# The first heads of a fused attention and mixture-of-experts kernel: another order of score products, zeroings on GpSimd, and a first head scored from 64 rows

## The chip, the cores and the metric

The kernel runs on one core of one Trainium2 chip. A core has TensorE (PE: matrix products and transposes, with a weight load ahead of each), VectorE (DVE), ScalarE (ACT), GpSimd (POOL) and SyncE (SP, which issues most transfers). The metric is the device time of one execution in microseconds, as a median of several executions; lower is better.

## What is computed

The reference, cut to what matters: causal attention of 4 batches with 12 heads, 448 rows and 64 columns a head, and then a mixture of 8 experts over the 1792 rows of 768 that come out.

```python
scores = scale * np.matmul(q, k.transpose(0, 1, 3, 2))
mask = np.triu(np.ones((seq, seq), dtype=bool), k=1)
scores = np.where(mask, -1000000000.0, scores)
scores = scores - np.max(scores, axis=-1, keepdims=True)
attn = np.exp(scores)
attn = attn / (np.sum(attn, axis=-1, keepdims=True) + 1e-09)
x = np.matmul(attn, v)                     # then rows of 768 for the experts
...
logits = x @ w_gate + modality_bias[modality_id]
e_idx = np.argmax(logits, axis=1)          # one expert for each row
out[mask] = gate_w[mask, None] * (np.maximum(x[mask] @ w1[e], 0.0) @ w2[e])
```

## The kernel before

The attention is a pipeline over 48 heads that is written out by hand: `iteration(n)` issues, in program order, the scores of head n, the exponentials of head n-1, the transposes and the split of head n-2, the second product of head n-3 and the sum of its two parts for head n-4. Each engine runs its own instructions in that order and waits for the others by semaphores. Heads come in pairs m = n // 2 (one load of q and k holds two heads, 64 rows each) and in groups of 4 (one load of V).

**Two kinds of heads.** Most heads are split into a high and a low part on GpSimd and stacked by transfers (`split_qk`, `split_kl`, `stack_qk`). The first eight, and the last two, are "plain": `first_load` brings q and k as they are, and the scores are computed with 128 rows, where q's rows of the other head of the pair are zeros. Those zeros are written ahead (`first_view(m, a)` is head a's q of pair m). A plain product runs as two passes.

**Scores.** `st_scores` computes four blocks of query rows: 64, 128, 128 and 128 rows with 64, 192, 320 and 448 columns, numbers 0 to 3. `SPOS` puts blocks 3 and 0 into bank `sa`, blocks 1 and 2 into bank `sb`. There is one bank of each, so a head can write `sa` only when DVE has taken up the head before. `SORD` is the order of the products: 3, 1, 0, 2 for plain heads. `ORD` is the order in which DVE takes the blocks (mask and row maximum, written to `p`): 3, 0, 1, 2. The exponentials on ACT follow DVE block by block.

**Second product.** `st_split` copies the transposed probabilities on ACT (`ph`) and takes the rest on DVE (`pl`); `st_pv` begins with two products of `ph` and goes on with those of `pl`. V is split as well: `split_vh` on GpSimd, `split_vl` for the first group on DVE and for the others on GpSimd. Groups 0 and 1 of V use the same buffer `vraw`, so `load_v(1)` waits until group 0 is split.

**The rest of the start.** 32 warm-up products of ones precede the first head on PE. Zeroings are shared out between DVE and GpSimd; some are put off into the first iterations by `later(n, f)`: `xg`, and parts of `sl` and `lt`. `clear_tables` issues four transfers of 160 KB. All transfers but the first half of q go through SyncE's queue, in program order, and each waits by its semaphore until the one eight issues ahead of it has landed.

Of the kernel before, what the change touches and what calls it, by code (L numbers as in the profile page):

```python
# [21 lines left out]
def attention_moe(  # L22
# [11 lines left out]
    nc = tc.nc  # L34
    V = nc.vector
    P = nc.gpsimd
    A = nc.scalar
    B, HP, _, _, S = qk.shape
# [3 lines left out]
    E, _, DF = w1.shape  # L42
# [3 lines left out]
    GH = 4  # L46
# [28 lines left out]
    def bank(tag, bufs=1):  # L75
        return ps.tile([128, 512], F32, tag=tag, name=tag, bufs=bufs)

    def sm(shape, tag, dt=F32, bufs=2):
        return small.tile(shape, dt, tag=tag, name=tag, bufs=bufs)

    def cst(name, shape, dt=F32):
        return const.tile(shape, dt, name=name)
# [16 lines left out]
    lts = [ltp[:, j] for j in range(2)]  # L99
    sls, pes = ([cst(f"{x}{j}", [128, NTL, E + 1]) for j in range(2)] for x in ("sl", "pe"))  # L100
# [31 lines left out]
    xg = [early.tile([128, DM], F32, name=f"xg{j}") for j in range(2)]  # L132
# [18 lines left out]
    def T(shape, dt, tag, bufs):  # L151
        return atp.tile(shape, dt, tag=tag, name=tag, bufs=bufs)
# [27 lines left out]
    raw, spl, vhl, sc, prob, pt, xrow, rec, lt_all, cx, rt, ov, ol = ({} for _ in range(13))  # L180
# [43 lines left out]
    def first_view(m, c):  # L224
        k, j = (
            ((3, 0), (3, 1), (4, 0)), ((2, 0), (2, 1), (4, 1)),
            ((0, 0), (0, 1), (1, 0)), ((5, 0), (5, 1), (1, 1)),
        )[m][c]
        return raw1[k][:, j * S:(j + 1) * S]

    def first_load(m):
        nc.sync.dma_start(out=first_view(m, 2), in_=qk[0, m, :, 1])
        for a in range(2):
            r = slice(a * 64, a * 64 + 64)
            (nc.sync if m or a else nc.scalar).dma_start(out=first_view(m, a)[r], in_=qk[0, m, r, 0])
            spl[2 * m + a] = (first_view(m, a), first_view(m, 2), None, None)

    LATE = (23,)

# [15 lines left out]
    def v_of(gr):  # L255
        return vraws[gr > 1 and gr % 2 == 0]

    def load_v(gr):
        b, u = divmod(gr, NG)
        c = slice(u * GH * D, (u + 1) * GH * D)  # L260
        t = v_of(gr)
        nc.sync.dma_start(out=t[:, 0:3, :], in_=v[b, 0:384, c].rearrange("(t p) c -> p t c", p=128))
        nc.sync.dma_start(out=t[64:128, 3, :], in_=v[b, 384:448, c])

    def vsrc(gr):
        return v_of(gr).rearrange("p t (h d) -> p t h d", h=GH)

    def split_vh(gr):
        t = T([128, NTL, GH, 2, D], F32R, "vhl", 2)
        P.tensor_scalar(out=t[:, :, :, 0], in0=vsrc(gr), scalar1=1.0, scalar2=0.0, op0=ALU.mult, op1=ALU.add)  # L270
        vhl[gr] = t

    def split_vl(gr, eng):
        t = vhl[gr]
        eng.tensor_tensor(out=t[:, :, :, 1], in0=vsrc(gr), in1=t[:, :, :, 0].bitcast(F32), op=ALU.subtract)

    SPOS = [(0, 448), (1, 0), (1, 192), (0, 0)]
    ORD = (3, 0, 1, 2)
    SORD = ((3, 0), (3, 1), (1, 0), (0, 0), (0, 1), (1, 1), (2, 0), (2, 1))

    def st_scores(g):
        qs, ks, qh, kl = spl.pop(g)
        banks = [bank("sa"), bank("sb")]
        nm = sm([128, NTL], "nm")
        p = praw[g % 3]

        outs, parts = {}, []
        for i, last in SORD:
            q0, n = QT[i]
            w = q0 + n  # L290
            bk, c0 = SPOS[i]
            if not last:
                outs[i] = banks[bk][:n, c0:c0 + w]
            if last and qh is None:
                continue
            a, z = (qh, kl) if last else (qs, ks)
            r = 128 if qh is None else n
            z0 = (128, 64, 64, 0)[i]
            nc.tensor.matmul(
                banks[bk][:r, c0:c0 + w], lhsT=a[:, q0:q0 + r], rhs=z[:, z0:z0 + w],  # L300
                start=(last == 0), stop=(last == 1 or qh is None),
            )
        for i in ORD:
            n = QT[i][1]
            w = QT[i][0] + n
            parts.append((i, n, outs[i], masks[i][:n], p[:n, POFF[i]:POFF[i] + w]))
        for i, n, o, m, z in parts:
            V.tensor_tensor_reduce(  # L308
                out=z, in0=o, in1=m, scale=-scale, scalar=3.0e38, op0=ALU.add, op1=ALU.min,
                accum_out=nm[:n, i:i + 1],  # L310
            )
        sc[g] = (p, parts, nm)
# [143 lines left out]
    def st_norm(gr, i):  # L456
        norm_l(gr, i)
        norm_x(gr, i)
# [472 lines left out]
    with tc.manual_schedule():  # L931
        for m in range(2):
            first_load(m)
# [5 lines left out]
            out=bias_sb.rearrange("p m o e -> p (m o e)"),  # L939
            in_=mod_bias.rearrange("(o m) e -> o (m e)", o=1).to_broadcast([128, NM * E]),  # L940
# [1 line left out]

        V.memset(ones, 1.0)
        warm_bank = bank("x")
        for _ in range(32):
            nc.tensor.matmul(warm_bank[:, 0:128], lhsT=ones, rhs=ones, start=True, stop=True)
        warm = sm([1, 1], "warm")
        V.memset(warm, 0.0)
        for m in range(3):
            for a in range(2):  # L950
                (P if m == 2 else V).memset(first_view(m, a)[64 - a * 64:128 - a * 64], 0.0)
        A.activation(out=warm, in_=warm, func=AF.Exp)
        P.memset(mask12, 0.0)
        P.affine_select(
            out=mask12[:, 384:512], in_=mask12[:, 384:512], compare_op=ALU.is_ge, fill=-1e9,
# [55 lines left out]
        def later(n, f):  # L1011
            todo.setdefault(n, []).append(f)
# [9 lines left out]
                f()  # L1022

        for j in range(2):
            later(2 * j, lambda j=j: V.memset(xg[j], 0.0))
            later(1 + j, lambda j=j: V.memset(sls[j][64:128, 0, E:E + 1], 1.0e6))
            later(1 + j, lambda j=j: V.memset(lts[j][64:128, 0], 0.0))

        def fma(o, x, mul, add):
            P.tensor_scalar(out=o, in0=x, scalar1=mul, scalar2=add, op0=ALU.mult, op1=ALU.add)  # L1030
# [120 lines left out]
        def iteration(n):  # L1151
            split = 7 < n + 3 < NHEAD and n + 3 >> 1 not in LATE
            ahead = n + 5 >> 1 in LATE
            if n % 2 == 1 and split and not ahead:
                stack_qk((n + 3) // 2)
            gr, i = divmod(n - 2 * GH, GH)
            comb = 0 <= gr < B * NG
            if 0 <= n - 4 < NHEAD:
                st_out(n - 4)
            if comb:  # L1160
                st_move(gr, i)
                st_norm(gr, i)
                b, u = divmod(gr, NG)
                if u == NG - 1:
                    later(n + 1, lambda i=i: x_store(b, i))
                    if i == NTL - 1:
                        after_batch(b, n)
            run_todo((n,))
            if n in (2, 3):
                st_trans(n - 2)  # L1170
            if n < NHEAD:
                st_scores(n)
            if n % 2 == 1 and ahead:
                late_load((n + 5) // 2)
                stack_qk((n + 3) // 2)
            run_todo(n)
            if n == 0:
                split_vh(0)
            if n % 2 == 1 and split:
                split_kl((n + 3) // 2)  # L1180
            if n % 2 == 0 and 7 < n + 4 < NHEAD:
                (late_zeros if n + 4 >> 1 in LATE else split_qk)((n + 4) // 2)
            if n % GH == 1 and n > GH:
                st_sums(n // GH - 1)
            if n % GH == RECAT and n > GH:
                st_rec(n // GH - 1)
            if 0 <= n - 1 < NHEAD:
                st_exp(n - 1)
            if 0 <= n - 2 < NHEAD:
                if n > 3:  # L1190
                    st_trans(n - 2)
                run_todo(-n)
                st_split(n - 2)
            if 0 <= n - 3 < NHEAD:
                st_pv(n - 3)
                st_low(n - 3)
            gr, i = divmod(n - 2 * GH + 1, GH)
            if 0 <= gr < B * NG:
                st_comb(gr, i)
            if n == 1:  # L1200
                split_vl(0, V)
            if n == 2 or n % GH == 3 and n > GH and n // GH + 1 < B * NG:
                split_vh(n // GH + 1)
            if n == 2 or n % GH == 0 and n > GH:
                split_vl((n + 2) // GH, P)
            if n == 4:
                V.memset(vraws[1][0:64, 3, :], 0.0)
            if n in (1, 3, 5, 7):
                load_qk(4 + n // 2)
            if n % 2 == 0 and n > 7 and n + 8 < NHEAD and n + 8 >> 1 not in LATE:  # L1210
                load_qk((n + 8) // 2)
            if n in (1, 4):
                load_v(n // GH + 1)
            if n == 1:
                clear_tables()
            if n % GH == 2 and n > GH and n // GH + 2 < B * NG:
                load_v(n // GH + 2)
# [51 lines left out]
        n = NHEAD  # L1269
# [263 lines left out]
```

## Time and profile before

| | |
|---|---|
| median of 3 runs | 483.30 us |
| lowest, highest | 483.16, 484.15 us |
| the profiled execution | 483.15 us |
| its span (first to last instruction) | 481.4 us |
| PE busy in the span | 466.1 us (97%) |
| DVE, ACT, GpSimd busy | 291.1, 278.0, 236.3 us |

A profile is one execution. Busy time of PE is modelled from pipelined products, so two neighbouring products overlap in the rows; what a product costs is read from start to start. A row of the timeline merges equal instructions in a row and says at its end how long the engine was idle before it, if it was, and what the idle time is put down to.

### The profile page before, as it was taken

The numbers are of one execution on the slowest core, as the hardware profiler recorded it, in microseconds if no ns is written. First come the engines' busy times: TensorE is split into PE (matmuls) and PEld (weight loads), VectorE is DVE, ScalarE is ACT, GpSimd is POOL, SyncE is SP. The second block draws the span as 40 slices with busy tenths as digits, with TensorE's granted clock in tenths as the row PEclk, the third lists the DMA queues.
The fourth block names the chain that finished last, engine by engine and source line by source line (L and its number), as shares of the span: only waits on it lengthen the run. The fifth ranks groups of instructions, "written<-read, shape, count | busy, mean of one in ns | idle before, by whom it ended". The sixth has DMA issues, their size and how long they took to land. (4 is left out here: it accounts for less than half of the span.)

```text
span 481.4 us, 10091 instructions
## 1 busy us (share of the span) xinstructions
PE 466.1 (97%) x3219; PEld 430.2 (89%) x3219; DVE 291.1 (60%) x860; ACT 278.0 (58%) x696; POOL 236.3 (49%) x319
## 2 busy tenths in 40 slices
PE   8999999999999999989999999999999999999992
PEld 6789998999899888779999999999999999889772
DVE  7999999999999998797211126620130120194392
ACT  6899999999999996243312125620220211384591
POOL 7997999999998999852202004002001001020231
PEclk9999999999999999999999999999999999999997
DMA  7799799998986795623693006833001002075400
GB/s 193 227 252 264 199 233 284 244 230 227 261 237 160 180 284 204 204 72 100 215 403 108 33 1 229 303 127 102 34 0 56 34 1 67 33 249 195 152 15 4
DMA packets 43302, 77.24 MB, mean 160 GB/s; under 512 B 15582, under 2 KB 27614, under 8 KB 43232
## 3 DMA queue, kind: packets, MB, share of 16 engines
q1 hardware_dynamic: 40112, 65.30, 47.8%
q0 software_dynamic: 3040, 11.03, 6.6%
q8 instruction: 27, 0.44, 0.4%
q14 instruction: 43, 0.35, 0.2%
q10 hardware_dynamic: 80, 0.11, 0.1%
HBM read 48.10 MB, written 12.08 MB: 125 GB/s over the span
## 5 line engine op out<-in xcount | busy, mean ns | idle before, releaser
L786 POOL DMA_INDIRECT xg<-xs,idg x18 | 21.0, 1169 | 156.5 <-DVEq L1439 81.1
L318 ACT ACTIVATE p<-p,nm 128x448 f32<-128x448 f32 x192 | 94.8, 497 | 1.5 <-DVE nm L308 1.5
L824 DVE SCALAR_TENSOR_TENSOR htl<-g,hth 128x256 fp32r<-128x256 f32 x40 | 16.7, 424 | 104.6 <-ACT hth L823 104.6
L805 PE MATMUL g<-xh,w1h 128*128 128x256 f32 x240 | 67.1, 279 | 0.4 <-DVE htl L824 0.4
L807 PE MATMUL g<-xh,w1l 128*128 128x256 f32 x240 | 67.2, 280 | 0.0
L806 PE MATMUL g<-xl,w1h 128*128 128x256 f32 x240 | 67.0, 279 | 0.0
L348 DVE TENSOR_TENSOR pl<-pt,ph 128x1024 fp32r<-128x1024 f32 x48 | 58.3, 1216 | 4.6 <-ACT ph L347 4.0
L361 PE MATMUL ot<-ph,vhl 128*128 128x448 f32 x192 | 50.1, 302 | 1.9 <-DVE ut L392 1.0
L823 ACT ACTIVATE hth<-g 128x256 fp32r<-128x256 f32 x40 | 15.1, 383 | 63.2 <-PE g L807 60.3
L347 ACT ACTIVATE ph<-pt 128x1024 fp32r<-128x1024 f32 x48 | 49.1, 1022 | 2.6 <-PE pt L330 1.8
L330 PE MATMUL pt<-ident,p 128*128 128x128 f32 x384 | 49.8, 273 | 0.0
L330 PEld LDWEIGHTS pt<-ident,p 128*128 128x128 f32 x384 | 44.8, 141 | 2.1 <-issue 0.2
L805 PEld LDWEIGHTS g<-xh,w1h 128*128 128x128 f32 x240 | 44.9, 187 | 0.6 <-DVE htl L824 0.6
L806 PEld LDWEIGHTS g<-xl,w1h 128*128 128x128 f32 x240 | 45.1, 188 | 0.0
L865 POOL DMA_INDIRECT out_dram<-row,idg x14 | 16.0, 1142 | 59.3 <-ACTq L1423 29.5
L807 PEld LDWEIGHTS g<-xh,w1l 128*128 128x128 f32 x240 | 45.1, 188 | 0.0
L361 PEld LDWEIGHTS ot<-ph,vhl 128*128 128x128 f32 x192 | 32.8, 189 | 5.8 <-DVE ut L392 2.0
L308 DVE CUSTOM_DVE_ANT_0 p<-sa,mask 128x448 f32<-128x448 f32 x96 | 36.2, 413 | 1.0 <-ACT wi L980 0.5
L308 DVE CUSTOM_DVE_ANT_0 p<-sb,mask 128x192 f32<-128x192 f32 x96 | 36.3, 413 | 0.0
L318 ACT ACTIVATION_READ_ACCUMULATOR p<-p,nm 128x1 f32 x192 | 36.3, 189 | 0.0
L368 PE MATMUL ot<-pl,vhl 128*64 128x64 f32 x192 | 34.6, 295 | 0.5 <-DVE pl L348 0.4
L392 DVE TENSOR_TENSOR ut<-ot,hol 64x448 f32<-64x448 f32 x48 | 29.4, 612 | 1.4 <-ACT hol L386 0.7
(381 smaller groups left out, 1294.4 us busy)
## 6 DMA issues: line engine op xcount, KB each, us to landing
raw<-in_moe_w_dram SPq DMA_DIRECT2D x24, 512.0 KB
st<-hl SPq DMA_DIRECT2D x52, 224.0 KB
raw<-in_qk_dram SPq DMA_DIRECT2D x19, 448.0 KB
raw<-in_moe_w_dram SPq DMA_DIRECT2D x20, 384.0 KB
vraw<-in_v_dram SPq DMA_DIRECT2D x7, 384.0 KB
w1h<-hl SPq DMA_DIRECT2D x12, 224.0 KB
w1l<-hl SPq DMA_DIRECT2D x12, 224.0 KB
xs<-row SPq DMA_DIRECT2D x6, 384.0 KB
```

Source lines behind the costliest of these rows:

```text
L308: V.tensor_tensor_reduce(out=z, in0=o, in1=m, scale=-scale, scalar=3.0e38, op0=ALU.add, op1=ALU.min, accum_out=nm[:n, i:i + 1],)
L318: A.activation(out=z, in_=z, func=AF.Exp, bias=nm[:n, i:i + 1], scale=-1.0, accum_out=sums[:n, b, i, h:h + 1],)
L330: nc.tensor.transpose(out=o, in_=a, identity=ident)
L347: A.activation(out=ph, in_=t, func=AF.Copy)
L348: V.tensor_tensor(out=pl, in0=t, in1=ph.bitcast(F32), op=ALU.subtract)
L361: nc.tensor.matmul(o[:, q0:q0 + c1 - c0], lhsT=t[:, n, h].rearrange("p a d -> p (a d)"), rhs=ph[:, c0:c1], start=(n == 0), stop=(n == 1),)
L368: nc.tensor.matmul(o[0:D, q0:q0 + c1 - c0], lhsT=t[:, n, h, 0], rhs=pl[:, c0:c1], start=False, stop=False)
L392: V.tensor_tensor(out=ots(gr, j)[a * 64:a * 64 + 64], in0=ov.pop(g)[0:64, :S], in1=ol.pop(g), op=ALU.add)
L786: P.indirect_dma_start(out=xg[u][:n], out_offset=None, in_=xs[0:rows, :], in_offset=bass.IndirectOffsetOnAxis(ap=g[:n, 0:1], axis=0), boun ...
L805: nc.tensor.matmul(o, lhsT=ah, rhs=bh, start=first, stop=False)
L806: nc.tensor.matmul(o, lhsT=ah, rhs=bl, start=False, stop=False)
L807: nc.tensor.matmul(o, lhsT=al, rhs=bh, start=False, stop=last)
```

## The change

- The plain heads compute their four blocks in the order 3, 0, 1, 2 (`SPLAIN`), so first both blocks of `sa`, then both of `sb`.
- The first head is scored from 64 rows of q and k. Its transfer of k is cut in two: rows 0 to 63 go through SyncE's queue first, rows 64 to 127 through ACT's queue behind q's first half. The zeroing of the rows that the first head no longer reads is dropped. Five warm-up products are dropped (32 to 27).
- The zeroings of `xg`, `sl` and `lt` in iterations 0 to 2 go from DVE to GpSimd.
- `split_vl(0)` on DVE moves from the end of iteration 1 to iteration 2, behind the scores of head 2, and `load_v(1)` moves with it, behind the four table clearings.

```diff
     def first_load(m):
-        nc.sync.dma_start(out=first_view(m, 2), in_=qk[0, m, :, 1])
+        lead = slice(0, 64) if m == 0 else slice(0, 128)
+        nc.sync.dma_start(out=first_view(m, 2)[lead], in_=qk[0, m, lead, 1])
         for a in range(2):
             r = slice(a * 64, a * 64 + 64)
             (nc.sync if m or a else nc.scalar).dma_start(out=first_view(m, a)[r], in_=qk[0, m, r, 0])
-            spl[2 * m + a] = (first_view(m, a), first_view(m, 2), None, None)
+            if m == a == 0:
+                rest = slice(64, 128)
+                nc.scalar.dma_start(out=first_view(m, 2)[rest], in_=qk[0, m, rest, 1])
+            k = lead if a == 0 else slice(0, 128)
+            spl[2 * m + a] = (first_view(m, a)[k], first_view(m, 2)[k], None, None)
...
+    SPLAIN = ((3, 0), (0, 0), (1, 0), (2, 0))
...
-        for i, last in SORD:
+        for i, last in SPLAIN if qh is None else SORD:
...
-            if last and qh is None:
-                continue
...
-        for _ in range(32):
+        for _ in range(27):
...
             for a in range(2):
-                (P if m == 2 else V).memset(first_view(m, a)[64 - a * 64:128 - a * 64], 0.0)
+                if m or a:
+                    (P if m == 2 else V).memset(first_view(m, a)[64 - a * 64:128 - a * 64], 0.0)
...
-            later(2 * j, lambda j=j: V.memset(xg[j], 0.0))
-            later(1 + j, lambda j=j: V.memset(sls[j][64:128, 0, E:E + 1], 1.0e6))
-            later(1 + j, lambda j=j: V.memset(lts[j][64:128, 0], 0.0))
+            later(2 * j, lambda j=j: P.memset(xg[j], 0.0))
+            later(1 + j, lambda j=j: P.memset(sls[j][64:128, 0, E:E + 1], 1.0e6))
+            later(1 + j, lambda j=j: P.memset(lts[j][64:128, 0], 0.0))
...
+            if n == 2:
+                split_vl(0, V)
+                load_v(1)
...
-            if n == 1:
-                split_vl(0, V)
...
-            if n in (1, 4):
-                load_v(n // GH + 1)
+            if n == 4:
+                load_v(2)
```

Three places show what now stands where. First PE, from the last warm-up product to the middle of the second head (`raw_119` is k, `raw_118` is q of the first pair). Before:

```order
L946 MATMUL x<-ones 128x128
L299 MATMUL sa<-raw_119,raw_118 128x448
L299 MATMUL sb<-raw_119,raw_118 128x192
L299 MATMUL sa<-raw_119,raw_118 128x64
L299 MATMUL sb<-raw_119,raw_118 128x320
L299 MATMUL sa<-raw_119,raw_118 128x448
```

And of the change:

```order
L950 MATMUL x<-ones 128x128
L303 MATMUL sa<-raw_119,raw_118 128x448
L303 MATMUL sa<-raw_119,raw_118 128x64
L303 MATMUL sb<-raw_119,raw_118 128x192
L303 MATMUL sb<-raw_119,raw_118 128x320
L303 MATMUL sa<-raw_119,raw_118 128x448
```

The 64 columns of `sa` have moved ahead of the 192 of `sb`; the next head's first product again writes `sa`. Second, DVE from the last block of head 1 (`p_156`) to the low part `pl` of head 0 (`p_157` is head 2; the rows `nm` store the row maximum). Before:

```order
L308 ISA p_156,nm<-sb,mask_158 128x320
L308 ISA nm 128x1
L1026 MEMSET sl_86 64x1
L1027 MEMSET ltp 64x112
L275 TENSOR_TENSOR vhl<-vraw,vhl 128x16x64
L308 ISA p_157,nm<-sa,mask 128x448
...
L308 ISA p_157,nm<-sb,mask_158 128x320
L308 ISA nm 128x1
L1025 MEMSET xg_128 128x768
L1026 MEMSET sl_87 64x1
L1027 MEMSET ltp 64x112
L348 TENSOR_TENSOR pl<-pt,ph 128x1024
```

And of the change:

```order
L312 ISA p_156,nm<-sb,mask_158 128x320
L312 ISA nm 128x1
L312 ISA p_157,nm<-sa,mask 128x448
...
L312 ISA p_157,nm<-sb,mask_158 128x320
L312 ISA nm 128x1
L280 TENSOR_TENSOR vhl<-vraw,vhl 128x16x64
L352 TENSOR_TENSOR pl<-pt,ph 128x1024
```

V's low part (`vhl`) has moved from ahead of head 2 to behind it, and the zeroings are gone from this queue. Third, SyncE's queue around V's second load (`vraw`). Before:

```order
L190 DMA raw_118<-in_qk_dram 128x896
L262 DMA vraw<-in_v_dram 128x3x256
L263 DMA vraw<-in_v_dram 64x256
L1144 DMA table_70<-row 128x320
L1144 DMA table_71<-row 128x320
L1144 DMA table_72<-row 128x320
L1144 DMA table_73<-row 128x320
L190 DMA raw_119<-in_qk_dram 128x896
```

And of the change:

```order
L190 DMA raw_118<-in_qk_dram 128x896
L1149 DMA table_70<-row 128x320
L1149 DMA table_71<-row 128x320
L1149 DMA table_72<-row 128x320
L1149 DMA table_73<-row 128x320
L267 DMA vraw<-in_v_dram 128x3x256
L268 DMA vraw<-in_v_dram 64x256
L190 DMA raw_119<-in_qk_dram 128x896
```

V's second load stands behind the four table clearings instead of ahead of them.

## Rows read from the trace of the kernel before

**Rows 1.** The head of the page.

```profile
span 481.4 us, 10091 instructions
```

**Rows 2.** Windows: length, each engine's busy us, granted clock, DMA share, GB/s.

```profile
0.00:5.00 5.00, 3.87 (x33) 3.83 (x34) 3.08 (x15) 2.47 (x7) 4.01 (x22) 1.00 0.54 153
...
60.00:80.00 20.00, 19.93 (x154) 18.17 (x153) 19.45 (x68) 19.73 (x58) 19.39 (x28) 1.00 0.94 242
```

**Rows 3.** Timeline of PE to 40 us: start, duration, instruction, idle time before it.

```profile
1.13 3.33 PEld L946 LDWEIGHTS <-ones 128*128 128x128 bf16 x32 [1.13 <-DVE warm L948]
...
4.52 1.26 PE L299 MATMUL sa<-raw,raw 128*128 128x448 f32 x2
...
5.94 0.33 PE L299 MATMUL sa<-raw,raw 128*128 128x64 f32 x2
...
7.29 0.99 PE L299 MATMUL sa<-raw,raw 128*128 128x448 f32 x2 [0.42 <-PE sb L299]
...
15.47 0.48 PE L368 MATMUL ot<-pl,vhl 128*64 128x64 f32 x2 [0.39 <-DVE pl L348]
...
16.22 0.96 PE L299 MATMUL sa<-raw,raw 128*128 128x448 f32 x2
...
19.98 0.91 PE L299 MATMUL sa<-raw,raw 128*128 128x448 f32 x2
20.73 0.49 PE L299 MATMUL sb<-raw,raw 128*128 128x192 f32 x2
...
21.82 1.04 PE L330 MATMUL pt<-ident,p 128*128 128x128 f32 x8
22.61 0.54 PE L361 MATMUL ot<-ph,vhl 128*128 128x448 f32 x2
...
38.71 0.46 PE L299 MATMUL sa<-st 128*128 128x448 f32 x1
```

**Rows 4.** Waits in PE's queue on the scores' line, from 3.5 to 4.5 us.

```profile
L299 PEldq EVENT_SEMAPHORE  x1: 364/364/364, 3.8 to 3.8; - x1
```

**Rows 5.** Timeline of DVE from 4 to 16 us.

```profile
4.89 0.99 DVE L975 MEMSET raw<- 64x448 f32 x2
6.42 0.62 DVE L308 CUSTOM_DVE_ANT_0 p<-sa,mask 128x448 f32<-128x448 f32 x1 [0.53 <-ACT wi L980]
...
10.54 1.23 DVE L275 TENSOR_TENSOR vhl<-vraw,vhl 128x1024 fp32r<-128x1024 f32 x1
...
11.68 0.62 DVE L308 CUSTOM_DVE_ANT_0 p<-sa,mask 128x448 f32<-128x448 f32 x1
...
12.37 0.35 DVE L308 CUSTOM_DVE_ANT_0 p<-sb,mask 128x192 f32<-128x192 f32 x1
...
13.24 0.70 DVE L1025 MEMSET xg<- 128x768 f32 x1
...
14.19 1.23 DVE L348 TENSOR_TENSOR pl<-pt,ph 128x1024 fp32r<-128x1024 f32 x1
...
15.33 0.61 DVE L308 CUSTOM_DVE_ANT_0 p<-sa,mask 128x448 f32<-128x448 f32 x1
```

**Rows 6.** Timeline of GpSimd to 44 us.

```profile
3.10 0.81 POOL L966 MEMSET wi<- 128x864 f32 x1
...
9.22 1.05 POOL L270 TENSOR_SCALAR vhl<-vraw 128x1024 fp32r<-128x1024 f32 x1 [1.33 <-DMA vraw<-in_v_dram]
...
10.70 1.18 POOL L1045 TENSOR_TENSOR gt<-row,gt 128x32 f32<-128x32 f32 x1
...
17.55 1.05 POOL L270 TENSOR_SCALAR vhl<-vraw 128x1024 fp32r<-128x1024 f32 x1
...
43.48 0.24 POOL L441 TENSOR_TENSOR ltp<-cxt,rec 128x32 f32<-128x32 f32 x1 [3.22 <-ACT cxt L432]
```

**Rows 7.** Timeline of SyncE's queue: the table clearings, and eight issues behind head 10's stack.

```profile
13.29 2.33 SPq L1144 DMA_DIRECT2D table<-row  x4
...
35.00 0.91 SPq L215 DMA_DIRECT2D w1l<-hl  x1
```

## The prediction

> **What bounds the kernel now.** I read the views in this order: the page's head, the windows, then the timeline of the first 40 us engine by engine, and last the waits. The span is 481.4 us [rows 1] and the profiled execution took 483.15 us, so 1.75 us lie outside the span; the median of the three runs is 483.30 us, 0.15 us above the profiled one. In the middle of the attention nothing has slack: from 60 to 80 us PE is busy for 19.93 of 20 us, ACT for 19.73, DVE for 19.45 and GpSimd for 19.39 [rows 2]. There the heads follow each other at a pace that this change hardly touches. The change works on the first 17 us, where PE does wait, so what it can give is a shift: if head 4 starts earlier by some time and nothing later is late, the whole rest starts earlier by that.
>
> So I look at what stands between the start and head 4 [rows 3]. A head of this stage ("plain" scores) costs PE 1.84 us when nothing waits (head 5: 19.98 to 21.82), of which the product of 448 columns takes 0.75 (19.98 to 20.73); its transposes take 0.79 (21.82 to 22.61). Before head 4 begins, at 16.22 us, three things are lost:
> - The two passes of the very first product take 1.26 us (from 4.52) where head 5's take 0.91. The windows give a granted clock of 1.00, the upper level, for 0 to 5 us [rows 2], so they do not say why; passes at half rate until about 5.2 us would give it (twice 0.35 behind 4.52).
> - Head 1 starts at 7.29 after 0.42 us in which PE sat idle. It must write the bank `sa`, which DVE is still reading: DVE took up `sa` at 6.42 [rows 5], because the last product into `sa` (64 columns, at 5.94) stood behind one into `sb`.
> - The low part of head 0's second product waits 0.39 us, until 15.47, for `pl`, which DVE began at 14.19 behind a zeroing of `xg` (13.24) and, earlier, V's low part (10.54, 1.14 us until the next instruction) [rows 5].
>
> From 16.22 us on the rows of PE carry no idle time in this stage.
>
> **The change part by part, with the sum.**
> *Start.* Five warm-up products fewer: 32 of them take 3.33 us of weight loads [rows 3], 0.104 us each, so 0.52 us. PE could begin head 0 at 4.00 instead of 4.52. Its queue, however, waited for the semaphores of head 0's operands until 3.8 + 0.364 = 4.17 us [rows 4]. Those were 336 KB (all of k, half of q); now head 0 needs 224 KB, from two queues. The q half still goes through ACT's queue as before, so the landing may not move at all. Bounds for the first product: 4.00 and 4.52; I take 4.20. With half rate until 5.2 that loses 0.50 us.
> *Bank by bank.* The products of `sa` (448 and 64 columns, 0.92 us by head 5 without the 192 between) now stand together. They are issued by 5.2 + 0.42 = 5.62. Before, DVE began 0.31 us after the last one was issued (5.94 + 0.17 to 6.42); so now at 5.93. DVE is free by then: its last zeroing, from 4.89 for 0.99 [rows 5], moves up by the one that is dropped (half of that, 0.50) and ends at 5.38. From DVE's start to head 1 took 0.87 us (6.42 to 7.29): head 1 starts at 6.80, and PE has issued head 0 by 4.20 + 1.84 + 0.50 = 6.54, so 0.26 us of idle time are left.
> *Head 1 and 2.* Head 1 until 8.64, transposes of head 0 until 9.43, head 2 from there. Its `sa` products are out at 10.35, DVE starts at 10.66 (before: 11.68). It would come to `sb` 0.69 us later (11.68 to 12.37), but those products are only ready at 9.43 + 1.84 + 0.31 = 11.58; then 0.87 us to the end of the head (12.37 to 13.24): 12.45.
> *DVE's queue behind it.* Before came `xg`, `sl` and `lt` (13.24 to 14.19, 0.95 us); these go to GpSimd. V's low part (1.14) moves in instead, from a place where it delayed head 2. So `pl` starts at 13.59 and the products that wait for it 1.28 later (14.19 to 15.47), at 14.87; they took 0.75 us to head 4 (15.47 to 16.22): **head 4 at 15.62, 0.60 us earlier**. The other path there, DVE taking up head 3 (15.33, 0.89 us ahead of head 4), gives 14.73 + 0.89 = 15.62 as well. With the bounds of the start it is 0.44 (at 4.52) to 0.70 (at 4.00).
>
> In this sum most of what the moved zeroings free on DVE is taken by V's low part; what remains comes from head 2 starting earlier. That DVE is packed from 11.58 on is why I do not expect more.
>
> *GpSimd takes the zeroings.* Two of 128x768; the nearest row is 0.81 us for 128x864, so 0.72 each [rows 6]. With the small ones (an estimate: a quarter of a us for each pair) I put them at 2.0 us. The first falls into the 1.33 us that GpSimd waited for V's first load. About 1.2 us are left, behind which stand the split of V's second group (before: 17.55) and of q and k for heads 8 to 11. GpSimd has 3.22 us of waiting ahead of 43.48, so it has caught up by then.
> *V's second load and the tables.* SyncE now issues the four table clearings (2.33 us, [rows 7]) ahead of V's second group, since its buffer is released by V's low part, at about 13.6. V lands some 2.3 us later, near 19; GpSimd would want it at 18.8. So its lag is 1.2 to 2 us. Who waits then? The stacks for head 10 are the tightest: in SyncE's queue each transfer waits for the one eight issues ahead, so the last stack of head 10 had landed by 35.00 [rows 7], and PE read it at 38.71 [rows 3]. Of these 3.7 us, 0.6 go to the earlier start and up to 2 to the lag: over 1 us remains. I cost this at nothing; without that cover, every us of lag beyond 3.1 costs one.
> *ACT's second DMA issue* stands ahead of its table load. ACT's first work for the chain is the mask, and DVE needs that only at 5.9; nothing, and at most the 0.5 us by which one issue of SyncE is spaced (2.33 for four) if the mask were late.
>
> One rule speaks for a cost. In the trace a small tensor operation of GpSimd (128x32) took 1.18 us at 10.70 [rows 6], while DVE ran V's low part from 10.54 to 11.77 [rows 5]; one of the same shape took 0.24 at 43.48. The Trainium skill, "SBUF — State Buffer", section "Who interferes with whom", says that GpSimd and DVE share a pair of ports, and that a DVE operation with two inputs from SBUF and a reading GpSimd operation exclude each other, the later waiting. By it the moved low part could itself wait for a short GpSimd operation, 0.24 us, and the sum would be 0.36. The row shows DVE's side unhurt, so I leave it at 0.60.
>
> **Time.** 483.15 - 0.60 = 482.55; against the median, 482.7. I say 482.6 us, 0.14% less.
>
> **The rivals.**
> *The slow passes end earlier (482.05).* If the half rate is gone by the first product, head 0's `sa` is out at 5.12, DVE starts at 5.43, head 1 at 6.30: 0.50 us more, 1.1 in all. For it: the rows do not say what the end of the slow passes hangs on. Against: the warm-up starts at the same time as before. Chance 0.2.
> *They end later (484.0), the other side.* The warm-up ends sooner and PE may idle some 0.2 us before head 0. If the half rate lasted until 8.6, head 0 would be issued at 7.88, head 1 by 10.08 and head 2 start at 10.87, 1.44 us later than in my sum: 0.84 us slower than before. It decides from about 6.4 us on, where the 0.60 us are used up; beyond 8.9 us the loss passes 0.2%. Against it: PE idled 0.42 and 0.39 us in this stage, and the first products of heads 1 and 4 right behind (0.99 and 0.96, head 5's 0.91) were not slow [rows 3]. Chance 0.1. The Trainium skill, "TensorE: Matmul & The Clock Gate", Part 1, says that the clock starts at half rate and that activity releases it, which speaks for this rival. No row here shows the lower level at the start, 1.2 GHz, so the trace neither agrees nor disagrees.
> *The shift is eaten (483.1).* ACT, nearly full from 60 us on [rows 2], loses no work by the change. If its pace and not PE's start sets the heads, 0.6 us at head 4 become waiting somewhere. For it: the busy shares are level. Against: ACT's exponentials follow PE's scores by way of DVE, so in the first heads ACT starts earlier with PE. Chance 0.13.
> *The stacks of head 10 come late (483.5 and more).* It needs a lag of GpSimd and SyncE above 3.1 us where I find 2. Chance 0.05.
>
> **How the numbers follow.** My forecast has 0.52, with a spread of its own from 482.3 to 482.9. A measurement of this kernel tells a change from none at about 0.2%, 0.97 us, so the forecast itself counts as no change. Faster by more: the first rival and a little of the forecast, 0.26. Slower by more: most of the second rival and part of the fourth, 0.10. The rest, 0.64, is within 0.2%. The range goes from the first rival, less some for the spread between runs (483.16 to 484.15 before), to the second: 481.6 to 484.0.
>
> **What would show it.** Head 0's first product near 4.2 and DVE taking up `sa` near 5.9; head 1 near 6.8 with about 0.3 us of idle PE; head 2 near 9.4; V's low part right behind head 2 on DVE and `pl` near 13.6; head 4 near 15.6. GpSimd's split of V's second group starts between 18.7 and 19.6, and PE shows no wait for stacks at heads 8 to 11. The prediction is wrong if head 4 is early by 0.6 and the end is not, if the first passes are slow beyond 5.2 us, or if any of heads 8 to 11 waits.

## The result, and the profile after

The changed kernel takes **486.7 us** (median of 6 executions, 486.40 to 487.01) where the kernel before takes 483.7 us beside it (6 executions, 483.16 to 484.49): a ratio of 1.0063 with a 95% interval of 1.0053 to 1.0073. It is slower by 0.6%. The prediction said 482.6 us, within 481.6 to 484.0; the time lies outside that range, on the side to which it gave 0.10.

The head of the page of the profiled execution (486.86 us), which answers to [rows 1]; PE's line is busy us, share of the span, instructions:

```profile
span 484.8 us, 10084 instructions
...
PE 470.8 (97%) x3214; PEld 432.9 (89%) x3214; DVE 289.2 (60%) x853; ACT 278.2 (57%) x696; POOL 238.3 (49%) x325
```

The timeline of PE up to head 4, which answers to [rows 3] (start, duration, instruction, idle time before it; x4 takes the products of one bank together):

```profile
1.13 3.06 PE L950 MATMUL x<-ones 128*128 128x128 bf16 x27 [1.13 <-DVE warm L952]
4.12 2.18 PE L303 MATMUL sa<-raw,raw 64*128 64x448 f32 x4
6.09 2.02 PE L303 MATMUL sb<-raw,raw 64*128 64x192 f32 x4
8.04 2.18 PE L303 MATMUL sa<-raw,raw 128*128 128x448 f32 x4
10.01 2.02 PE L303 MATMUL sb<-raw,raw 128*128 128x192 f32 x4
11.83 1.28 PE L334 MATMUL pt<-ident,p 128*128 128x128 f32 x8
12.95 1.08 PE L303 MATMUL sa<-raw,raw 128*128 128x448 f32 x4
13.87 1.08 PE L303 MATMUL sb<-raw,raw 128*128 128x192 f32 x4
...
18.84 0.97 PE L303 MATMUL sa<-raw,raw 128*128 128x448 f32 x2
```

The reader is to see the distance from a `sa` row to the `sb` row behind it. In head 2 it is 0.92 us (12.95 to 13.87). In heads 0 and 1 the same columns take 1.97 us (4.12 to 6.09, 8.04 to 10.01), about twice as long (0.99 us for head 1 of e1 below, which is at the upper level): TensorE is at its lower level, 1.2 GHz, through all of the first two heads and into the transposes behind them, and at 2.4 GHz from head 2 on. Before, only the first two passes were slow [rows 3]. (The granted clock that the windows print is 1.00 for 0 to 15 us in both kernels, so here the level has to be read from durations.)

What follows from it stands on DVE, which answers to [rows 5]; the timeline of DVE:

```profile
6.45 0.62 DVE L312 CUSTOM_DVE_ANT_0 p<-sa,mask 128x448 f32<-128x448 f32 x1 [1.24 <-ACT wi L985]
...
10.26 0.62 DVE L312 CUSTOM_DVE_ANT_0 p<-sa,mask 128x448 f32<-128x448 f32 x1 [1.22 <-PE sa L303]
...
15.68 1.22 DVE L280 TENSOR_TENSOR vhl<-vraw,vhl 128x1024 fp32r<-128x1024 f32 x1
16.82 1.22 DVE L352 TENSOR_TENSOR pl<-pt,ph 128x1024 fp32r<-128x1024 f32 x1
```

DVE sits idle for over a microsecond at a time while PE is slow, and `pl` starts at 16.82 instead of 14.19 [rows 5]. Head 4 starts at 18.84, 2.62 us later than before (16.22). From there to head 47 (180.02 against 177.41) every head is 2.58 to 2.64 us late: nothing is added and nothing given back. The median is 3.0 us longer. The span of the profiled execution is 3.4 us longer; near its end, from 470 to 475 us, this one execution has a further stretch with a granted clock of 0.69, and its mean is 0.991 where the other five have 0.995 or 0.996. What makes the median 0.4 us longer than the shift of the heads is not traced.

GpSimd, which answers to [rows 6]; its timeline:

```profile
18.01 0.74 POOL L1030 MEMSET xg<- 128x768 f32 x1
...
20.96 1.05 POOL L275 TENSOR_SCALAR vhl<-vraw 128x1024 fp32r<-128x1024 f32 x1 [1.93 <-DMA vraw<-in_v_dram]
...
46.10 0.24 POOL L445 TENSOR_TENSOR ltp<-cxt,rec 128x32 f32<-128x32 f32 x1 [2.46 <-ACT cxt L436]
```

It rounds V's second group 3.41 us later than before (20.96 against 17.55), having waited 1.93 us for the load. As PE is late by 2.6 us itself, nobody waits for it here: before 46.10 it is idle for 2.46 us again.

### The profile page after: what moved, and what is told of

Same layout as the page of the kernel before. It is cut to its first block, busy times and chain, and to the rows that moved or that the text cites. A ratio compares the mean times of both kernels' runs of the same rounds, so it can differ in the third digit from the quotient of the medians.

```text
span 484.8 us, 10084 instructions
## 1 busy us (share of the span) xinstructions
PE 470.8 (97%) x3214; PEld 432.9 (89%) x3214; DVE 289.2 (60%) x853; ACT 278.2 (57%) x696; POOL 238.3 (49%) x325
```

## The experiments

Twelve kernels were run, in three groups, each beside the kernel before on the same chip (e5 to e8 on another chip than the rest). "Slow start" below means executions at 486 us or more, which the kernel before never had (93 executions beside the three groups, at most 484.51). They are counted by their times: of the slow ones only the changed kernel's and e10's were profiled.

### What keeps the first heads slow

The change does two things ahead of the first product: five warm-up products fewer, and products of head 0 over 64 rows of the contraction instead of 128. Two kernels take one of them out of the changed kernel, two put one alone into the kernel before.

**e1, changed kernel with 32 warm-up products:**

```
-        for _ in range(27):
+        for _ in range(32):
```

> The change with its five warm-up products back (32), all else as changed. Theory W (the shorter warm-up alone keeps PE at half rate until 12.3 us): the rate rises near 5 us, head 2 starts near 9.5 us, the time is 482.8 to 483.4 us. Theory R (the first head's 64-row products do not raise PE's rate, so it waits for head 1's 128-row products): the rise stays near 12 us, the first product of head 2 starts near 13 us, 486.4 to 487.2 us. Theory WR (only both together): as W.

Measured: 483.66 us (482.08 to 486.67, ten executions), ratio 1.0023 [1.0002, 1.0044]. Two of the ten were at 486.53 and 486.67, the others at 482.08 to 484.65. No theory holds as stated: R expected all of them slow, W and WR none.

**e2, changed kernel with the first head from 128 rows** (27 warm-up products, loads and zeroings of the first head as before):

```
-        lead = slice(0, 64) if m == 0 else slice(0, 128)
-        nc.sync.dma_start(out=first_view(m, 2)[lead], in_=qk[0, m, lead, 1])
+        nc.sync.dma_start(out=first_view(m, 2), in_=qk[0, m, :, 1])
...
-            spl[2 * m + a] = (first_view(m, a)[k], first_view(m, 2)[k], None, None)
+            spl[2 * m + a] = (first_view(m, a), first_view(m, 2), None, None)
```

> The change with the first head from 128 rows again (one transfer of k, the zeroing back), but 27 warm-up products. W: slow passes as in the change, 486 us or more. R: the rise comes near 5 us as before, head 4 starts near 15.7 us, 482.8 to 483.4 us. WR: as R.

Measured: 482.95 us (482.44 to 484.82), ratio 1.0000 [0.9986, 1.0014]. No slow start in ten. PE's timeline:

```profile
4.15 2.15 PE L298 MATMUL sa<-raw,raw 128*128 128x448 f32 x4
6.10 1.24 PE L298 MATMUL sb<-raw,raw 128*128 128x192 f32 x4
7.32 1.16 PE L298 MATMUL sa<-raw,raw 128*128 128x448 f32 x4
8.32 1.13 PE L298 MATMUL sb<-raw,raw 128*128 128x192 f32 x4
```

The first bank is at the lower level here too (1.95 us, 4.15 to 6.10), but head 1 is at the upper one (1.00 us, 7.32 to 8.32). Head 4 starts at 16.08, not at the expected 15.7.

**e3, kernel before with 27 warm-up products** (`range(32)` becomes `range(27)`):

> The kernel before with 27 warm-up products instead of 32, nothing else. W: slower by 2.5 to 3.5 us, about 486.5 us. R and WR: within 0.5 us of before, 483.2 to 484.2 us. A theory that blames the order of the products or the moved zeroings also expects no change here.

Measured: 482.66 us (482.24 to 483.67), ratio 0.9994 [0.9985, 1.0004], against 483.05 us beside it. No slow start in ten. So the shorter warm-up alone costs nothing, and that theory falls.

**e4, kernel before with the first head from 64 rows** (the first hunk of the change, with the zeroing that it drops; 32 warm-up products):

> The kernel before with the first head from 64 rows (two transfers of k, one zeroing less), 32 warm-up products, the old order. W and WR: no slow heads, 483.2 to 483.9 us. R: two slow heads, the rise near 12 us, 486 to 487 us. A theory that blames the order or the zeroings expects no change.

Measured: 483.55 us (482.53 to 487.21), ratio 1.0034 [1.0009, 1.0060]. Four of ten at 486.21 to 487.21. Neither "64 rows alone" nor "only both" holds as stated: with 64 rows the slow start comes in some executions, and with the 27 warm-up products besides in all six.

**e8, changed kernel with 40 warm-up products** (`range(27)` becomes `range(40)`):

> The changed kernel with 40 warm-up products instead of 27, first head from 64 rows. With 27 all executions were slow at the start (486.4 to 487.0), with 32 two of ten. Theory WR (the longer the warm-up runs into the first head, the surer the clock rises; the 64-row products only fail to carry it): with 40 no execution is at 486 or more; head 0 starts 0.8 to 1.0 later than with 32 (5.4 to 5.7), head 4 at 16.4 or so, GpSimd's lag as before, time 483.4 to 484.4. Rival R (64-row products hold the clock down whatever runs ahead of them): some executions at 486 or more, as with 32.

Measured: 484.39 us (482.63 to 487.07), ratio 1.0032 [1.0015, 1.0050]. One execution at 487.07 and four more between 484.89 and 485.82, for which no profile shows the cause. A longer warm-up does not make it sure; the theory that it would falls. Whether it makes the slow start rarer, ten executions do not tell.

**e10, changed kernel with the first head's loads and zeroings as before, and products over 64 rows.** Against e2 this is one slice:

```
-            spl[2 * m + a] = (first_view(m, a), first_view(m, 2), None, None)
+            k = slice(0, 64) if m == a == 0 else slice(0, 128)
+            spl[2 * m + a] = (first_view(m, a)[k], first_view(m, 2)[k], None, None)
```

> The changed kernel with the first head's loads and zeroings as before, and 27 warm-up products, but the products of head 0 over the first 64 rows alone. Rows theory: as the changed kernel, head 0's and head 1's banks at half rate (sa to sb about 1.95), head 2 near 12.9, every execution or nearly every one at 486 or more. Loads theory: no execution at 486 or more, time about 483.0, head 2 at 10.2 or earlier.

Measured: 485.04 us (482.36 to 487.03), ratio 1.0025 [0.9999, 1.0051]. Five of ten at 486.04 to 487.03, the other five at 482.36 to 484.04. The profiled one is slow; PE's timeline:

```profile
4.19 2.18 PE L299 MATMUL sa<-raw,raw 64*128 64x448 f32 x4
6.16 2.02 PE L299 MATMUL sb<-raw,raw 64*128 64x192 f32 x4
8.11 2.18 PE L299 MATMUL sa<-raw,raw 128*128 128x448 f32 x4
10.08 2.02 PE L299 MATMUL sb<-raw,raw 128*128 128x192 f32 x4
```

The same 1.97 us in heads 0 and 1 as in the changed kernel. As nothing but the rows of the products differs from e2, which had no slow start, the rows are a cause, and the loads theory (none slow) falls. That it is five of ten and not nearly all says that the loads have a part in it too, or chance.

**e9, the other way round: the changed kernel's loads, products over 128 rows** (the other half of q zeroed again):

```
-            k = lead if a == 0 else slice(0, 128)
-            spl[2 * m + a] = (first_view(m, a)[k], first_view(m, 2)[k], None, None)
+            spl[2 * m + a] = (first_view(m, a), first_view(m, 2), None, None)
```

> The changed kernel with its loads of the first head as changed (64 rows on each of two queues, 27 warm-up products), but the products of head 0 over all 128 rows, whose other half of q is zeroed. Rows theory (products over 64 rows keep TensorE at half rate): heads 1 and on run at full rate (heads 1 to 2 start 2.7 to 2.9 apart instead of 4.9), no execution at 486 or more, time 482.6 to 483.8, the late V with it. Rival, loads theory (the earlier or split arrival of the data is the cause): as the changed kernel, every execution at 486 or more. Rival, chance theory (the 27 warm-ups are at the edge and the data's arrival decides): some at 486 or more.

Measured: 485.78 us (484.87 to 486.71, four executions), ratio 1.0049 [1.0030, 1.0068]. PE's timeline shows that it did not test what it was made for:

```profile
6.28 1.16 PE L302 MATMUL sa<-raw,raw 128*128 128x448 f32 x4 [2.08 <-DMA raw<-in_qk_dram]
7.27 1.59 PE L302 MATMUL sb<-raw,raw 128*128 128x192 f32 x4
8.65 2.02 PE L302 MATMUL sa<-raw,raw 128*128 128x448 f32 x4
10.47 1.41 PE L302 MATMUL sb<-raw,raw 128*128 128x192 f32 x4
```

The products over 128 rows need the half of k that comes last, through ACT's queue, and PE sat idle for 2.08 us ahead of them. They then began at the upper level (0.99 us from `sa` to `sb`, 6.28 to 7.27) and fell to the lower one during head 0's `sb` (head 1: 1.82 us, 8.65 to 10.47). Head 4 is 2.26 us late, of which head 0's late start is 1.76; the lower level shows in the distance from head 1 to head 2, 3.94 us where the kernel before has 2.78. So full products behind an idle stretch came to the lower level as well, in this one profile. On the rows it decides nothing.

### Where the shift of 0.60 us goes when the start is fast

e1's profiled execution has a fast start, and so shows the rest of the change. PE, DVE and GpSimd of e1, in three fences:

```profile
4.65 1.22 PE L303 MATMUL sa<-raw,raw 64*128 64x448 f32 x4
...
15.57 1.13 PE L303 MATMUL sa<-raw,raw 128*128 128x448 f32 x4
...
46.06 0.44 PE L303 MATMUL sa<-w1h 128*128 128x448 f32 x1 [0.46 <-DMA w1h<-hl]
...
54.04 0.44 PE L303 MATMUL sa<-st 128*128 128x448 f32 x1 [0.89 <-DMA st<-hl]
...
132.44 0.47 PE L303 MATMUL sa<-st 128*128 128x448 f32 x1 [0.29 <-DVE nm L312]
```

```profile
13.55 1.22 DVE L352 TENSOR_TENSOR pl<-pt,ph 128x1024 fp32r<-128x1024 f32 x1
...
131.52 0.19 DVE L511 TENSOR_REDUCE m<-eq 128x4 f32<-128x36 f32 x1 [0.74 <-POOL eq L508]
```

```profile
19.94 1.05 POOL L275 TENSOR_SCALAR vhl<-vraw 128x1024 fp32r<-128x1024 f32 x1 [0.82 <-DMA vraw<-in_v_dram]
...
42.09 0.94 POOL L195 TENSOR_SCALAR hl<-raw 128x896 fp32r<-128x896 f32 x1 [1.55 <-DMA raw<-in_qk_dram]
```

Head 4 starts at 15.57, 0.65 us early, and heads 8 to 11 are 0.70 early. Then it is lost: head 12 waits 0.46 us for its stack (in the buffer `w1h`) and head 14 another 0.89, after which heads 16 to 34 are 0.14 to 0.22 late. At head 35 DVE waits 0.74 us for a GpSimd operation of the batch's routing, and with that heads 36 to 47 are 0.90 to 0.97 late. GpSimd is behind all three: it rounds V's second group 2.39 us late (19.94 against 17.55 [rows 6]), and its stacks go out as much later. SyncE issues the load of the next q and k behind them, 2.58 us late. SyncE's timeline before and in e1, in two fences:

```profile
30.95 1.98 SPq L190 DMA_DIRECT2D raw<-in_qk_dram  x2
```

```profile
33.53 1.79 SPq L190 DMA_DIRECT2D raw<-in_qk_dram  x2
```

So GpSimd waits 1.55 us for that load at 42.09, and nothing is left of the 3.22 us that it had to spare before 43.48 [rows 6]. e2 shows the same steps at heads 14 and 35, from 0.14 early to 0.50 late. The step at head 14 is undone there by head 16 (0.38 late at head 14, 0.14 early at head 16); what stays falls at head 35.

GpSimd's timeline shows why that head decides; before, e1 and e6 (described below), in three fences:

```profile
130.34 0.25 POOL L504 TENSOR_TENSOR eq<-eq,e8v 128x32 f32<-128x32 f32 x1
```

```profile
44.21 0.24 POOL L445 TENSOR_TENSOR ltp<-cxt,rec 128x32 f32<-128x32 f32 x1
...
131.24 0.25 POOL L508 TENSOR_TENSOR eq<-eq,e8v 128x32 f32<-128x32 f32 x1
```

```profile
42.33 0.24 POOL L440 TENSOR_TENSOR ltp<-cxt,rec 128x32 f32<-128x32 f32 x1 [0.96 <-ACT cxt L431]
...
129.16 0.24 POOL L503 TENSOR_TENSOR eq<-eq,e8v 128x32 f32<-128x32 f32 x1
```

Between these two operations GpSimd's rows show less than 0.7 us of idle time in all, in each of the fourteen profiles. So what it is early or late by at the first (43.48 before) it carries to the second (130.34 before), which DVE needs at head 35; in every profile the shift of head 36 is that of the second row, to 0.01 us. Where GpSimd still waits for ACT at the first row (e3 to e7, e9, e10 and the changed kernel), it is as early or late as the heads are, and their shift is kept. Where the wait for q and k has used up that idle time (e1, e2, e8, e11, e12), GpSimd's own shift replaces theirs: 0.90 us late in e1, where the heads had been 0.70 early.

Three kernels take e2 apart, by the two things that reach GpSimd: the zeroings, and V's first low part with V's second load.

**e5, e2 with the zeroings back on DVE:**

```
-            later(2 * j, lambda j=j: P.memset(xg[j], 0.0))
+            later(2 * j, lambda j=j: V.memset(xg[j], 0.0))
```

(and the `sl` and `lt` lines in the same way)

> The changed kernel with its first head from 128 rows (so the clock rises early), and the xg, sl and ltp zeroings back on VectorE; V's first low part and second load stay late. Compared with the same kernel with the zeroings on GpSimd (first run of 128 rows: GpSimd rounds V of group 2 at 19.46 after 1.04 us of waiting for V's load, head 14 waits 0.26 for its stack, head 35 waits for VectorE, heads 36 to 47 start 0.50 late against before, span 481.9). Theory M (GpSimd starts that rounding when the later of two things is there, its own queue or V's second load, and V's load is the later): the rounding still starts at 19.2 to 19.7, with the wait for the load grown to 2 us or more, heads 36 to 47 still 0.35 to 0.60 late, span 481.7 to 482.1. Rival Z (the two microseconds of zeroings on GpSimd are the lag by themselves): the rounding starts at 17.4 to 17.7, heads 36 to 47 within 0.15 of before, span 481.2 to 481.5.

Measured: 483.55 us (482.73 to 484.38), ratio 1.0007 [0.9998, 1.0017]. GpSimd's timeline:

```profile
19.78 1.06 POOL L270 TENSOR_SCALAR vhl<-vraw 128x1024 fp32r<-128x1024 f32 x1 [1.85 <-DMA vraw<-in_v_dram]
```

The rounding starts no earlier than in e2 although GpSimd has two microseconds of zeroings less; the wait for the load has grown from 1.04 to 1.85 us. So V's load is the later of the two, theory M (its two ranges are missed by 0.08 and 0.15 us). The end (heads 36 to 47 late by 0.31) comes by another road than expected, however: no wait for a stack here, but a late head 4. DVE's timeline:

```profile
12.44 0.70 DVE L1024 MEMSET xg<- 128x768 f32 x1
...
13.39 1.23 DVE L275 TENSOR_TENSOR vhl<-vraw,vhl 128x1024 fp32r<-128x1024 f32 x1
14.54 1.22 DVE L347 TENSOR_TENSOR pl<-pt,ph 128x1024 fp32r<-128x1024 f32 x1
```

With the zeroings and V's low part both ahead of `pl`, head 4 starts at 16.56, though head 3 was 0.56 early.

**e6, e2 with V's first low part and second load back at head 1, ahead of the tables:**

```
-            if n == 2:
-                split_vl(0, V)
-                load_v(1)
...
+            if n == 1:
+                split_vl(0, V)
...
-            if n == 4:
-                load_v(2)
+            if n in (1, 4):
+                load_v(n // GH + 1)
```

> The changed kernel with its first head from 128 rows, and V's first low part and second load back in the iteration of head 1, ahead of the tables; the zeroings stay on GpSimd. Theory M: the load is no longer the later, GpSimd's rounding of V of group 2 starts when its own queue lets it, at 18.2 to 18.7 with less than 0.2 of waiting for the load; the lag is then 0.7 to 1.1 instead of 1.9, which the slack at heads 14 and 35 takes up: no wait for a stack, heads 36 to 47 between 0.25 early and 0.10 late, span 481.1 to 481.5, time 482.4 to 483.2. Rival Z: the zeroings keep the lag, heads 36 to 47 still 0.35 or more late, span 481.7 or more.

Measured: **482.33 us** (481.86 to 483.42), ratio 0.9986 [0.9977, 0.9996]: faster than both kernels, by 0.14% against the kernel before. GpSimd's and PE's timelines:

```profile
18.61 1.05 POOL L270 TENSOR_SCALAR vhl<-vraw 128x1024 fp32r<-128x1024 f32 x1
```

```profile
12.27 1.08 PE L298 MATMUL sa<-raw,raw 128*128 128x448 f32 x4
...
15.11 1.08 PE L298 MATMUL sa<-raw,raw 128*128 128x448 f32 x4
```

GpSimd no longer waits for the load, its lag is 1.06 us (0.06 in e7, without the zeroings), no head waits for a stack, and head 4 is 1.11 us early. 0.52 of that head 3 has already (12.27; head 0 itself starts 0.47 early in this execution), 0.59 come between head 3 and head 4. It is kept to the end: heads 36 to 47 are 1.16 to 1.20 early, more than either theory expected. That the zeroings alone keep the end late (rival Z) falls.

**e7, both back** (which is the kernel before with bank by bank and 27 warm-up products):

> The kernel before with the scores of the first heads bank by bank and 27 warm-up products: first head from 128 rows, zeroings on VectorE, V's parts in their old places. Both theories: GpSimd's rounding of V of group 2 starts at 17.4 to 17.7 as before, no waits at heads 14 and 35. Bank by bank gives VectorE the first bank of heads 0 and 1 sooner, but heads 2 to 4 stand behind VectorE's queue and the zeroings in it: head 4 at 16.15 to 16.35 (before 16.22), heads 36 to 47 within 0.15 of before, time 482.4 to 483.2, no change that can be told. If bank by bank alone were what moves head 4, head 4 would be at 16.0 or earlier.

Measured: 482.53 us (481.79 to 483.52), ratio 0.9988 [0.9979, 0.9998]. Its profiled execution (483.03 us) has head 4 at 16.27 and no waits at heads 14 and 35, as expected (heads 36 to 47 are 0.13 to 0.19 late); its median is not to be told from e6's. Where its half microsecond comes from, this profile does not show, so of e6's 0.76 us no more than the part between heads 3 and 4 is traced to the zeroings.

The distance from head 3 to head 4 does not depend on the start, and sorts these kernels. It is 3.43 us before, 3.46 in e3, 3.41 in e7 (zeroings on DVE, V early); 2.84 in e6 (zeroings on GpSimd, V early); 3.21 in e2, 3.18 in e1 and in the changed kernel (zeroings on GpSimd, V late); 4.33 in e5 (zeroings on DVE, V late). Moving the zeroings gains 0.57 us there; moving V's low part behind head 2 gives 0.37 of it back.

**e11, e6 with 32 warm-up products** (`range(27)` becomes `range(32)`):

> The kernel with the best median so far (first head from 128 rows, bank by bank, zeroings on GpSimd, V's parts in their old places: 482.33, ratio 0.9986) with 32 warm-up products instead of 27. Theory W0 (the length of the warm-up is worth nothing between 27 and 32 where the products have 128 rows): 482.1 to 482.9, head 0 0.2 to 0.6 later, head 4 at 15.1 to 15.8. Rival: the longer warm-up makes the rate rise sooner in more of the executions, time below 482.2.

Measured: 482.86 us (482.03 to 483.45) beside 483.5, ratio 0.9985 [0.9976, 0.9994]. The same gain as e6 with another warm-up. Its profiled execution, though, lost part of the shift (1.25 early at heads 12 and 13, about 0.42 at 36 to 47); GpSimd's timeline:

```profile
40.74 0.94 POOL L195 TENSOR_SCALAR hl<-raw 128x896 fp32r<-128x896 f32 x1 [1.62 <-DMA raw<-in_qk_dram]
```

SyncE issued this load at 32.15, and the same one in e6 at 32.32, where GpSimd had it without a wait at 39.19. So the transfer itself took longer in e11. The DMA engines are full in this stretch in both (share 1.04 and 1.05 from 30 to 45 us); why this load landed later, the traces do not show.

**e12, e6 with the banks in the old order** (the kernel before with the zeroings on GpSimd and 27 warm-up products):

```
-        for i, last in SPLAIN if qh is None else SORD:
+        for i, last in SORD:
...
+            if last and qh is None:
+                continue
```

> The kernel before with 27 warm-up products and the zeroings on GpSimd alone: the banks of the first heads in the old order, V's parts in their old places. Theory: the gain of the best version (head 4 0.59 earlier against head 3, and kept to the end) is that of the zeroings taken off VectorE's queue ahead of head 4, and the order of the banks is worth nothing: head 4 less head 3 at 2.75 to 2.95 (before 3.43, best version 2.84), time 482.1 to 482.9. Rival: bank by bank is needed for it, as it lets VectorE start heads 0 and 1 sooner: head 4 less head 3 at 3.2 or more, time 482.7 to 483.5.

Measured: 483.06 us (482.64 to 483.48), ratio 0.9994 [0.9985, 1.0003]; head 3 to head 4 takes 2.90 us. The theory holds for that distance (bank by bank is not needed for it). That the order of the banks is worth nothing does not hold: PE's timelines of e11 and e12 show it ahead of that distance, in two fences:

```profile
4.52 1.22 PE L298 MATMUL sa<-raw,raw 128*128 128x448 f32 x4
...
6.75 1.16 PE L298 MATMUL sa<-raw,raw 128*128 128x448 f32 x4
```

```profile
4.14 0.99 PE L299 MATMUL sa<-raw,raw 128*128 128x448 f32 x2
...
6.64 0.99 PE L299 MATMUL sa<-raw,raw 128*128 128x448 f32 x2 [0.43 <-PE sb L299]
```

From head 0 to head 1 it takes 2.23 us bank by bank and 2.50 in the old order, 0.43 of it idle. In e12 head 0 runs at the upper level throughout, in e11 from almost its first product on, so the level does not make the difference. The time is at the upper edge of the expectation and lies between no change and e6. In the profiled execution the shift of 1.07 us at head 4 is lost again, with a wait of GpSimd for q and k as in e11 (2.01 us) and waits for the stacks of heads 12 and 14.

## Why the prediction was wrong

*The start.* The step that failed is "With half rate until 5.2 that loses 0.50 us". It carried the end of the slow passes over from the trace of before, while the change put other products there. The first product itself came as predicted (4.12, forecast 4.20). From there on the slow level lasted until the transposes of head 0, so `sa` was taken up at 6.45 (5.93), head 1 started at 8.04 (6.80), head 2 at 12.95 (9.43), `pl` at 16.82 (13.59) and head 4 at 18.84 (15.62): 3.2 us off, where the median is 4.1 us off the forecast; 0.4 of the rest is the kernel before itself, 483.7 us beside the change and 483.3 in the prediction. (In the sum for the start, 3.8 + 0.364 is 4.16 and not 4.17, which changes nothing.)

The rival "They end later" had the direction and the mechanism of the loss, but neither its cause nor its size. Its half rate ended at 8.6 us for a loss of 0.84; it ended beyond 11.8. It argued from PE's idle time ahead of head 0. The changed kernel's row at 4.12 has none, while e3, e5 and e7 idled there for 0.18 to 0.26 us and were not slow. The cause that e2, e4 and e10 show is another: products over 64 rows. With 128 rows and PE fed, no execution of e2, e3, e5, e6, e7, e11 and e12 had a slow start (0 of 78). With 64 rows it came in 2 of 10 (e1), 4 of 10 (e4), 1 of 10 with four more in between (e8), 5 of 10 (e10) and 6 of 6 (the changed kernel). I had counted the 64 rows only as half the bytes to load. Nor is 5.2 us a fixed end over 128 rows: the first bank took 1.95 us in e2 and 1.05 in e11. The argument against this rival, that PE's waits of 0.4 us later in the stage left the rate alone, was true and beside the point. The Trainium skill, "TensorE: Matmul & The Clock Gate", Part 1, says that the clock starts at half rate and that activity releases it; the trace after agrees, with 1.97 us from `sa` to `sb` in heads 0 and 1 and 0.92 in head 2. Why some executions with 64 rows rise in time and others not, and what part the earlier loads have in the six of six, stays open.

*Bank by bank, head 1 and 2, DVE's queue.* Where the start was fast the sum held: in e1 `pl` starts at 13.55 (forecast 13.59) and head 4 at 15.57 (15.62). In part that was luck: head 0 began 0.45 us later than forecast there (4.65) and lost next to nothing to slow passes, where 0.50 was forecast. "Most of what the moved zeroings free on DVE is taken by V's low part" holds as well: 0.37 of 0.57 us. Of the bank order itself the distance from head 3 to head 4 shows no gain (3.41 in e7 against 3.46 in e3); its gain is at head 1, 0.27 us from e12 to e11. There head 1 starts 2.23 us behind head 0, where the sum has 2.10 without slow passes.

*GpSimd and V's second load.* Costed at nothing, and wrong, though hidden in the changed kernel by its own late PE. The lag was put at 1.2 to 2 us and measured at 1.91 (e2) and 2.39 (e1). (The landing "near 19" does not follow from the 13.6 and 2.3 us that it names, which make 15.9; it came near 19.46 in e2.) "GpSimd has caught up by then" is the sentence that failed: the lag delays the load of q and k queued behind the stacks, and GpSimd's idle time ahead of 43.48 went into waiting for it. The cover failed elsewhere than where I looked: the stacks of head 10 were in time, those of heads 12 and 14 were not, and the loss that stays came at head 35. The rival "The stacks of head 10 come late" had the kind of loss with the wrong head and too high a threshold. By the prediction's own measure, the lag plus what the heads are earlier by, it expected a loss beyond 3.7 us; e1 lost with 3.1, e12 with 2.4, e11 with 2.2 and e2 with 2.05, while e6 with 2.2 and e5 with 1.9 lost nothing. So no single threshold sorts them; what does is whether GpSimd had to wait for q and k until its idle time was gone, and why it had to in e11 and not in e6 is not settled. That V's load and not the zeroings is the later of the two is shown by e5 and e6.

*The shared ports.* The cost of 0.24 us that was weighed by the Trainium skill, "SBUF — State Buffer", section "Who interferes with whom", did not appear: V's low part took 1.22 us on DVE in the changed kernel and `pl` followed 1.14 us behind its start, as head 2 did before [rows 5]. It was again an operation of GpSimd beside it that was long (128x16 at 15.89, 1.15 us; the same at 15.03 took 0.29).

*The shift is eaten.* It was, in e1, e2, e11 and e12, but not by ACT's pace: GpSimd's lag ate it, for good at head 35.

## What to carry to other kernels

Price an edit to the first products of a kernel by what TensorE does at its start, and not by bytes and columns alone: fewer rows or an idle stretch there can leave whole heads at half the clock, and one timed execution can miss it, so look at several. When an engine far from the critical path becomes late, follow its queue, with every load that stands behind its results, to the next place where it is idle: what it has not made up there it carries on, here over more than twenty heads, to head 35, where DVE needs a result of it. A move that frees an engine should be tried without the moves that came with it: with the zeroings on GpSimd and V's parts left in place the kernel was 0.14 to 0.15% faster than before (e6, e11). That is little: e7, which has the zeroings on DVE, is not told apart from it.

## What the runs showed of the hardware

Matrix products over 64 rows right behind a warm-up of 27 full ones left TensorE at 1.2 GHz for all of the 64-row head and the full 128-row head behind it (1.97 us per bank against 0.92) in the profiled execution, and by their times in all six. The same program can start at either level from one execution to the next, by its times: five of ten in e10. And PE idle for 2.08 us (e9) resumed at the upper level (0.99 us per bank) and fell to the lower one during the first head (1.82 us in the next), with full products throughout.
